# A branch hint that names all five engines, in a kernel of linear attention, routed experts and a gated feed-forward

## The chip, the cores and the metric

The kernel runs on one core of a Trainium2 chip. The metric is the device time of one execution, in microseconds (us). Several runs are made and their median is taken.

## The reference

Three stages follow each other on 1536 tokens (2 sequences of 768) with 384 features:

- attention with a decaying state: for each of 8 heads, `y_t = r_t (state + u k_t v_t)` and then `state = w state + k_t v_t`;
- a mixture of 8 experts, one expert for a token, with a capacity of 384 tokens for an expert: `gate * (relu(x w1) w2)`, inner width 1024;
- a gated feed-forward, `(silu(x w_gate) * (x w_val)) w_out`, inner width 1536.

What the reference computes doesn't limit how many tokens an expert gets, up to its capacity, nor what the decay `w` is. The kernel is written for the usual case of both, and has a second form for the rest.

## The kernel before, in words

The kernel is a straight line of instructions for the usual case: attention in chunks of 128 tokens, experts with at most 224 tokens each (`BLK`), then the gated feed-forward (`gated`, lines 918 to 1004). Behind it, under a condition, stands the general form (`general`, line 1007), which computes everything once more token by token and block by block. The condition is one number, `rare_i`, that VectorE works out in line 829, soon after the routing: it is above 0 when an expert has more than 224 tokens or a decay lies outside 0.6 to 1.6. With the inputs that are timed it is 0, and the general form is jumped over.

The order of each engine's instructions is the order of the source, since the schedule is written by hand (line 78, `manual_schedule`). Where an engine's instruction stands in the source thus decides where it stands in that engine's queue. Each of the five engines has its own stream of instructions, and each of them has to take the same branch for itself: it loads `rare_i` into a register of its own (line 102, TENSOR_LOAD) and compares it (line 107, COMPARE_BRANCH).

The load and the mark for the hint are both in `at_end` (lines 101 to 103). `gated` calls it from line 970, in its last part: the last group of 384 tokens is gated (`inner`), then `outer` takes it in three tiles of 128 tokens. For each tile TensorE makes 36 matmuls into `po` (lines 965 to 967), VectorE adds `po` to `acc` (line 974), and GpSimd scatters the 128 finished rows to `out` (line 976, an indirect DMA through POOL's queue). `at_end` comes between the last tile's matmuls and that tile's addition:

```
967                    nc.tensor.matmul(po, lhsT=al[:, ts_], rhs=wh, start=False, stop=(i == len(parts) - 1))
968                n = g * NTT + tt
969                if n == NT - 1 and last:
970                    at_end()
974                    nc.vector.tensor_add(acc[:, n], acc[:, n], po)
976                    nc.gpsimd.indirect_dma_start(
```

So in TensorE's stream all matmuls stand ahead of the load of the flag, in VectorE's the last addition stands behind it, and in GpSimd's the last scatter does. ScalarE and SyncE (SP, the queue of the plain loads) have no work behind it. At each of these places the compare and branch is the next thing, but for that one addition and that one scatter.

`tc.If` is told to prefer the true branch as the next block (`preferred_fallthrough_block=True`), so the general form stands right behind the straight line in every engine's stream, and the usual case takes the branch over it, to a short block that waits for the last DMAs and to the program's end (line 1143 in the trace).

In the kernel before, line 103 calls `mark_branch_hint_location("rare", hint=0)`. `hint=0` says that the branch labelled `rare` is likely taken. The call names no engine, and the trace has no instruction of line 103 on any of them.

## Time and profile before

| what | value |
|---|---|
| median of 3 runs | 475.48 us (475.33 to 477.2) |
| the profiled execution's own time | 475.25 us |
| its span in the profile | 473.1 us |
| instructions in the span | 8116 |
| mean granted TensorE clock | 0.972 of full speed |
| VectorE, ScalarE, GpSimd busy | 66%, 45%, 38% of the span |

The span goes from the first to the last instruction of the program, and the execution's own time is 2.15 us longer. An engine's name with a "q" behind it (POOLq, PEldq) stands for the engine's sequencer, the part that waits, loads registers, branches and hands instructions on; its time isn't counted as busy. PEld is TensorE's weight load, whose sequencer is TensorE's.

### The profile page before, as it was taken

The page shows a single profiled execution, that of the slowest core. Times are in us where ns is not written, and L with a number is a line of the kernel's source. Part 1 is how long each engine was busy: PE and PEld are TensorE (multiplying, and loading weights), DVE is VectorE, ACT ScalarE, POOL GpSimd, SP SyncE. Part 2 cuts the span into 40 slices and gives each one's busy share as a digit, 9 for nine tenths or more (in the row PEclk, how much of TensorE's full clock was granted, in tenths as well). Part 3 has the DMA queues.
Part 4 walks back from the last instruction along what each step waited for, and adds up shares of the span by engine and source line. Part 5 has one row for each costly group of instructions (what it writes and reads, how often), then busy time and mean ns, then how long its engine had stood idle before and what let it go on. Part 6 is the DMA issues. An engine that isn't in the chain of part 4 may idle for free.

```text
span 473.1 us, 8116 instructions
## 1 busy us (share of the span) xinstructions
PE 448.0 (95%) x3028; PEld 434.8 (92%) x3028; DVE 311.0 (66%) x640; ACT 211.8 (45%) x474; POOL 179.3 (38%) x165
## 2 busy tenths in 40 slices
PE   7898997999999999999999999999999999999991
PEld 6787887889899999999999899999999999999991
DVE  6889899778877878888656787989858111111110
ACT  2556465345666575675554564444343122120310
POOL 6967756121111112010043454755544433233321
PEclk9599799999999999999999999999999999999997
DMA  7785781258989989960201234233310000101001
GB/s 263 245 279 194 247 266 38 74 188 275 346 258 298 234 244 252 303 229 1 68 0 68 78 124 133 73 128 110 100 60 0 34 19 1 51 0 40 11 19 39
DMA packets 24802, 63.78 MB, mean 135 GB/s; under 512 B 4784, under 2 KB 10032, under 8 KB 24752
## 3 DMA queue, kind: packets, MB, share of 16 engines
q1 hardware_dynamic: 22112, 57.43, 38.5%
q0 software_dynamic: 1920, 4.73, 2.8%
q10 hardware_dynamic: 720, 1.00, 0.7%
q8 instruction: 26, 0.43, 0.4%
q14 instruction: 24, 0.20, 0.1%
HBM read 55.67 MB, written 7.48 MB: 133 GB/s over the span
## 4 chain that ended last, share of the span: by engine, by line
PE 79%; DVE 13%; issue 2%; DMA 2%; ACT 1%; POOL 1%; POOLq 0%; DVEq 0%; ACTq 0%
PE A L730 12%; PE py L719 7%; PE g L945 5%; PE g L944 5%; PE g L943 5%; PE A L944 5%; PE A L945 5%; PE A L943 5%; PE po L967 5%; PE po L966 5%; PE po L965 5%; PE py L720 4%; PE A L259 3%; PE A L742 2%; DVE AT L265 2%
## 5 line engine op out<-in xcount | busy, mean ns | idle before, releaser
L952 POOL TENSOR_TENSOR al<-sg,ah 128x384 fp32r<-128x384 f32 x48 | 54.2, 1129 | 122.0 <-ACT ah L951 122.0
L585 DVE TENSOR_TENSOR wlo<-raw,whi 128x768 fp32r<-128x768 f32 x60 | 57.9, 965 | 10.6 <-ACT whi L584 10.0
L719 PE MATMUL py<-hc,whi 128*128 128x448 f32 x192 | 63.1, 370 | 0.0
L951 ACT CAST ah<-sg 128x384 fp32r<-128x384 f32 x48 | 24.7, 514 | 77.8 <-DVE sg L948 77.8
L730 PE MATMUL A<-xc,whi 128*128 128x224 f32 x336 | 57.3, 275 | 0.8 <-DVE xc L601 0.7
L720 PE MATMUL py<-hc,wlo 128*128 128x256 f32 x192 | 53.8, 280 | 0.0
L730 PEld LDWEIGHTS A<-xc,whi 128*128 128x128 f32 x336 | 51.1, 192 | 1.5 <-DVE xc L601 1.1
L584 ACT CAST whi<-raw 128x768 fp32r<-128x768 f32 x60 | 49.9, 838 | 0.7 <-PE py L719 0.7
L966 PE MATMUL po<-w_out_lo,ah 128*128 128x384 f32 x144 | 48.6, 337 | 0.0
L967 PE MATMUL po<-w_out_hi,al 128*128 128x384 f32 x144 | 48.6, 337 | 0.0
L965 PE MATMUL po<-w_out_hi,ah 128*128 128x384 f32 x144 | 48.5, 337 | 0.0
L730 PE MATMUL A<-xc,wlo 128*128 128x224 f32 x168 | 46.2, 275 | 0.0
L974 DVE TENSOR_TENSOR acc<-acc,po 128x384 f32<-128x384 f32 x36 | 19.2, 545 | 30.8 <-PE po L967 30.8
L719 PEld LDWEIGHTS py<-hc,whi 128*128 128x128 f32 x192 | 36.0, 188 | 2.5
L948 DVE TENSOR_TENSOR sg<-A,sg 128x384 f32<-128x384 f32 x24 | 13.3, 555 | 37.9 <-PE A L945 30.2
L720 PEld LDWEIGHTS py<-hc,wlo 128*128 128x128 f32 x192 | 36.5, 190 | 0.0
L795 POOL DMA_INDIRECT ids<-tok,by_expert x12 | 12.1, 1010 | 63.5 <-DMA ids<-tok,by_expert 63.2
L948 DVE TENSOR_TENSOR sg<-g,sg 128x384 f32<-128x384 f32 x24 | 13.3, 555 | 34.5 <-PE g L945 29.7
L253 ACT ACTIVATE AT<-ident,c 128x128 f32<-128x128 f32 x96 | 29.4, 389 | 8.8 <-DVE c L244 8.8
L749 ACT ACTIVATE hc<-A 128x224 fp32r<-128x224 f32 x64 | 23.1, 362 | 21.8 <-PE A L730 18.3
L730 PEld LDWEIGHTS A<-xc,wlo 128*128 128x128 f32 x168 | 32.3, 192 | 0.0
L947 ACT ACTIVATE sg<-A 128x384 f32<-128x384 f32 x24 | 11.7, 487 | 34.6 <-PE A L945 34.6
(166 smaller groups left out, 1185.5 us busy)
## 6 DMA issues: line engine op xcount, KB each, us to landing
raw<-in_w SPq DMA_DIRECT2D x62, 384.0 KB, 6.4
rkT<-in_rkT SPq DMA_DIRECT2D x12, 512.0 KB, 5.0
rk<-in_rk SPq DMA_DIRECT2D x12, 384.0 KB, 4.0
raw<-in_w_gate SPq DMA_DIRECT2D x6, 768.0 KB, 4.2
raw<-in_w_val SPq DMA_DIRECT2D x6, 768.0 KB, 4.3
raw<-in_w_out SPq DMA_DIRECT2D x6, 768.0 KB, 4.3
x_disp<-zero SPq DMA_DIRECT2D x8, 336.0 KB, 6.2
xr<-x_disp SPq DMA_DIRECT2D x8, 336.0 KB, 6.1
```

Source lines behind the costliest of these rows:

```text
L584: nc.scalar.copy(h_, raw)
L585: nc.vector.tensor_sub(l_, raw, h_.bitcast(F32))
L719: nc.tensor.matmul(ps[:, 0:2 * BLK], lhsT=wh, rhs=xc, start=first, stop=False, skip_group_check=True)
L720: nc.tensor.matmul(ps[:, 0:256], lhsT=wl, rhs=xc[:, 0:256], start=False, stop=last, skip_group_check=True)
L730: self.nc.tensor.matmul(ph[:, HI], lhsT=w[:, k, fs], rhs=x[1][:, k, half], start=(k == 0 and i == 0), stop=(k == KD - 1 and i == 2),)
L943: nc.tensor.matmul(pg[m], lhsT=wh[:, k, fs], rhs=xh[:, k], start=(k == 0), stop=False)
L944: nc.tensor.matmul(pg[m], lhsT=wh[:, k, fs], rhs=xl[:, k], start=False, stop=False)
L945: nc.tensor.matmul(pg[m], lhsT=wl[:, k, fs], rhs=xh[:, k], start=False, stop=(k == KD - 1))
L952: nc.gpsimd.tensor_sub(l_, sg, h_.bitcast(F32))
L965: nc.tensor.matmul(po, lhsT=ah[:, ts_], rhs=wh, start=(i == 0), stop=False)
L966: nc.tensor.matmul(po, lhsT=ah[:, ts_], rhs=wl, start=False, stop=False)
L967: nc.tensor.matmul(po, lhsT=al[:, ts_], rhs=wh, start=False, stop=(i == len(parts) - 1))
```

## The change

The hint names all five engines. By the change's own title the finished program then holds it. Nothing else is touched.

```diff
                 def at_end():
                     flag.append(nc.values_load(self.rare_i[0:1, 0:1], min_val=0, max_val=2))
-                    tc.mark_branch_hint_location("rare", hint=0)
+                    tc.mark_branch_hint_location("rare", hint=0, engines=[ET.Pool, ET.PE, ET.DVE, ET.SP, ET.Activation])
```

## Rows read from the trace of the kernel before

**Rows 1.** The page: TensorE's busy time, and the chain that ended last.
```profile
PE 448.0 (95%) x3028; PEld 434.8 (92%) x3028; DVE 311.0 (66%) x640; ACT 211.8 (45%) x474; POOL 179.3 (38%) x165
PE 79%; DVE 13%; issue 2%; DMA 2%; ACT 1%; POOL 1%; POOLq 0%; DVEq 0%; ACTq 0%
```

**Rows 2.** Timeline, last pieces: start us, duration us, engine, line, operation [idle before].
```profile
462.62 0.34 PE L967 MATMUL po<-w_out_hi,al 128*128 128x384 f32 x1
...
462.99 0.55 DVE L974 TENSOR_TENSOR acc<-acc,po 128x384 f32<-128x384 f32 x1 [2.59 <-PE po L967]
```

**Rows 3.** The chain that ended last, from 460 us: start us, duration us, what.
```profile
460.91 3.21 DMA out<-acc,idx
464.12 0.02 issue
464.14 0.02 POOLq L976
464.16 0.51 issue
...
464.89 0.96 POOL out L976
```

**Rows 4.** Line 107, branch and cleanup: ns min/median/max, first and last start us.
```profile
L107 SPq EVENT_SEMAPHORE  x8: 17/17/17, 346.3 to 346.9; - x8
L107 POOLq EVENT_SEMAPHORE  x5: 17/43/2841, 465.1 to 468.3; - x5
L107 DVEq EVENT_SEMAPHORE  x2: 21/21/21, 466.1 to 466.2; - x2
L107 SPq COMPARE_BRANCH  x1: 53/53/53, 342.2 to 342.2; - x1
L107 ACTq COMPARE_BRANCH  x1: 50/50/50, 454.7 to 454.7; - x1
L107 ACTq EVENT_SEMAPHORE  x1: 17/17/17, 457.5 to 457.5; - x1
L107 PEldq COMPARE_BRANCH  x1: 3936/3936/3936, 460.3 to 460.3; - x1
L107 DVEq COMPARE_BRANCH  x1: 72/72/72, 463.0 to 463.0; - x1
L107 PEldq EVENT_SEMAPHORE  x1: 51/51/51, 464.3 to 464.3; - x1
L107 POOLq COMPARE_BRANCH  x1: 45/45/45, 464.7 to 464.7; - x1
L107 POOLq INC_SWDGE_SEM  x1: 904/904/904, 468.4 to 468.4; - x1
```

**Rows 5.** Line 1143, the program's end, same columns.
```profile
L1143 POOLq DRAIN  x3: 40/107/3015, 469.3 to 472.9; - x3
...
L1143 DVEq EVENT_SEMAPHORE  x2: 21/21/21, 472.5 to 473.1; - x2
```

**Rows 6.** Line 102, each engine's load of the flag, same columns.
```profile
L102 SPq TENSOR_LOAD <-rare_i x1: 273/273/273, 341.6 to 341.6; - x1
...
L102 ACTq TENSOR_LOAD <-rare_i x1: 462/462/462, 454.2 to 454.2; - x1
L102 PEldq TENSOR_LOAD <-rare_i x1: 483/483/483, 459.7 to 459.7; - x1
L102 DVEq TENSOR_LOAD <-rare_i x1: 310/310/310, 459.9 to 459.9; - x1
L102 POOLq TENSOR_LOAD <-rare_i x1: 506/506/506, 460.7 to 460.7; - x1
```

**Rows 7.** Line 976, time to landing: all 12 scatters, then the last two alone.
```profile
DMA to landing us min/median/max: 2.6/2.6/3.2
...
DMA to landing us min/median/max: 3.2/3.2/3.2
```

**Rows 8.** Instruction packets while the last two scatters were under way (460.9:464.1, 464.7:468.2).
```profile
q8 instruction: 1, 0.02, 1.9%
...
q8 instruction: 1, 0.02, 2.2%
q14 instruction: 2, 0.02, 1.6%
```

**Rows 9.** The page's DMA queues: packets, MB, share of 16 engines over the span.
```profile
q8 instruction: 26, 0.43, 0.4%
q14 instruction: 24, 0.20, 0.1%
```

## The prediction

> **What bounds the kernel now.** The page comes first: TensorE is busy for 95% of the span, and the chain that ended last runs over it for 79% [rows 1]. Nothing that stands before the hint in any stream is touched, so the question is only what the end of the program waits for. I read that from the last pieces backwards. TensorE's last matmul starts at 462.62, VectorE's last addition runs from 462.99 to 463.54 [rows 2]. Yet the last scatter isn't issued then: GpSimd's sequencer still waits for the landing of the scatter before, at 464.12, and then takes 0.51 us to hand the last one on, which starts at 464.89 [rows 3]. It lands 3.2 us later, about 468.1 [rows 7]. Behind it come GpSimd's cleanup (INC_SWDGE_SEM, 468.4, 0.90 us [rows 4]) and its DRAIN from 469.3 of 3.02 us, to 472.3; only then are the others let go, at 472.5, and the span ends at 473.1 [rows 5]. From 460.9 on the end is a chain of POOL's queue and two scatters; no branch stands on it but GpSimd's own.

> Then the branches. What the hint could save is the time from an engine's branch to its first instruction behind it [rows 4]: SP 342.2 to 346.3, 4.1 us; ScalarE 454.7 to 457.5, 2.8; TensorE 3.94, here inside the branch itself; VectorE 463.0 to 466.1, 3.1; GpSimd 464.7 to 465.1, 0.4. I take the four long ones to be the fetch of the code behind the jump; GpSimd seems to have it at hand.

> **The change, part by part.** It adds one sequencer instruction to each stream, behind the load of the flag, and moves or removes nothing. If the hint starts the fetch at once, an engine gains the time between its hint and its branch:

> - SP, ScalarE and TensorE: the load ends at 341.9, 454.7 and 460.2 [rows 6], and the branch comes at 342.2, 454.7 and 460.3 [rows 4]. The lead is 0.3 us at most, so their waits of 4.1, 2.8 and 3.9 us stay nearly as they are.
> - VectorE: the load ends at 460.2, the branch waits behind the addition until 463.0. The lead of 2.8 us eats nearly the whole 3.1.
> - GpSimd: the load ends at 461.2, the branch comes at 464.7. The lead is 3.5 us, but only 0.4 is there to be saved.

> **What each saving is worth.** All of it ends in a wait. ScalarE, TensorE and VectorE are past the branch at 457.5, 464.3 and 466.1 [rows 4], and their next wait ends at 472.5 [rows 5]; the cover is 6.4 us for the latest of them. SP is past at 346.3 and then waits for the scatters' landings, over 120 us later. GpSimd's first 0.4 us lie inside its wait of 2.84 us for the last landing, which is the long one among the five semaphores [rows 4]. So 0 us for all five, and the cover that would have to go is that of GpSimd, 2.84 us.

> **What the added instructions cost.** The trace has no hint, so I bound it. Its nearest rows are the branches on the same sequencers, 0.045 to 0.072 us where the fetch isn't counted in; the far end is the branch that held its sequencer for 3.94 us [rows 4]. I take 0.05 us, since the hint only hands over the branch's target. At that price it is hidden everywhere. On VectorE it runs in the 2.8 us before the matmuls end, on GpSimd in the 2.9 us from 461.2 to 464.14 in which the sequencer waits for a landing [rows 3]. On TensorE every matmul was handed on before the load, on SP and ScalarE nothing is behind it but the branch. Queued behind the hint and waited for by others are only VectorE's addition (GpSimd waits for it) and GpSimd's scatter (the end does).

> **What the fetches touch.** The last two scatters land after 3.2 us, the median of the twelve is 2.6 [rows 7], and each of the two has a packet of instructions on q8 under way with it, the last one two more on q14 [rows 8]. If these packets are what delays them, moving them matters, and both scatters stand on the chain. The first delay is worth no more than 464.12 - 463.54 = 0.58 us, for then the addition is late next; the second 3.2 - 2.6 = 0.6. The gain is thus between 0 and 1.2 us. I take 0: both windows hold a packet of q8, the queue with the larger packets, and TensorE, the engine with most code, has a lead of only 0.1 us, so that its fetch falls where it fell. An added packet could in turn delay a scatter that isn't delayed now; there is none left among the two, so the bound above is one more delay of the same size, 0.6 us.

> **Sum.** 475.25 us (the profiled execution: 473.1 of span and 2.15 around it) - 0 + 0 = 475.25. The median of the runs is 0.23 above that execution; I give 475.4, between the two, as no change.

> [...] Instruction packets come in two sizes, 0.43 MB / 26 = 16 KB on q8 and 0.20 MB / 24 = 8 KB on q14 [rows 9]; what they displace no row shows. [...]

> **The rivals.**

> - *The change does nothing on the chip*: the instructions stand there, or not, and no fetch starts early. For it: line 103 has no row now. Time 475.4, as forecast. Chance 0.10, told apart only by VectorE's gap.
> - *The moved packets free the scatters*: VectorE's fetches shift by 2.8 us and the last scatter lands in 2.6 us, or both do. 475.25 - 0.6 = 474.65, at most 474.05. For it: 3.2 against 2.6. Against it: q8's packet stays in both windows. Chance 0.18.
> - *The hint holds its sequencer like a fetch*, the lighter one on the slow side. On GpSimd it would run from 461.2 for 3.94 us to 465.15, where the wait ended at 464.14: +1.0 us, 476.3 to 476.5. It decides where the hint takes over 2.9 us. Against it: four of the five branches are recorded at 0.05 to 0.07 us. Chance 0.07.
> - [...] Chance 0.06. [...]
> - *The end waits for code after all*: GpSimd's DRAIN of 3.02 us, or what lies around the span, shrinks as the code comes earlier: over 2.4 us faster, at most 475.25 - 3.0 = 472.2. For it nothing but the size of the DRAIN; it starts right behind a DMA cleanup on the same engine. Chance 0.04.

> **How the numbers follow.** My forecast, nothing moves on the chain, has the remaining 0.55, the rival that does nothing joins it at the same time. 0.5% is 2.4 us, about what a measurement of this kernel can tell from no change. Faster by more needs the last rival and a little of chance: 0.04. Slower by more needs the displaced code, with something for an unforeseen stall at the end: 0.07. The same: 0.89. The range goes from both scatters freed, 474.0, to the held sequencer on top of the median, 475.48 + 1.0, with 0.1 for the added instructions: 476.6. That leaves out the last two cases and little else.

> **What would show it.** Line 103 should have five rows of some 0.05 us: SP near 342, ScalarE near 454.7, TensorE near 460.2, VectorE near 460.2, GpSimd near 461.2. VectorE's first semaphore of line 107 should follow its branch within 0.5 us, not 3.1; TensorE's branch should stay above 3.5 us, SP's and ScalarE's gaps above 2.5. The issue of the last scatter should stay within 0.2 us of where the landing before it puts it, and the DRAIN at 3.0. I am wrong if GpSimd's last scatter starts more than 1 us later against the last matmul, if a hint row is longer than 1 us, or if the stretch from the last landing to the end shrinks.

## The result, and the profile of the changed kernel

The changed kernel is slower: 478.06 us against 475.29 us for the kernel before, medians of 20 runs each, ratio 1.0066 with a 95% interval of 1.0037 to 1.0095. That lies above the range that was given, 474.0 to 476.6 us. Ratios, here and below, leave out the executions over 1.5% above the fastest of their kernel; medians hold all of them. Single executions of either kernel spread widely (471.5 to 480.3 us before, 474.5 to 481.2 after), so that the two profiled ones, with spans of 473.1 and 473.6 us, hardly show the difference; what follows compares stretches inside them, and many runs for the times.

**The hints stand at the wrong end.** The trace has five new instructions. They carry line 1143, not 103, and they run at the very start. Rows of that line in the changed kernel (engine, count: ns min/median/max, first and last start in us):

```profile
L1143 POOLq BRANCH_PREFETCH_HINT  x1: 58/58/58, 0.8 to 0.8; - x1
L1143 ACTq BRANCH_PREFETCH_HINT  x1: 45/45/45, 0.8 to 0.8; - x1
L1143 SPq BRANCH_PREFETCH_HINT  x1: 51/51/51, 0.8 to 0.8; - x1
L1143 DVEq BRANCH_PREFETCH_HINT  x1: 57/57/57, 0.9 to 0.9; - x1
L1143 PEldq BRANCH_PREFETCH_HINT  x1: 50/50/50, 0.9 to 0.9; - x1
```

**What they did to the branches.** Line 107 in the changed kernel answers to [rows 4]:

```profile
L107 SPq EVENT_SEMAPHORE  x8: 17/17/17, 343.7 to 346.7; - x8
L107 POOLq EVENT_SEMAPHORE  x5: 17/43/2312, 466.1 to 468.7; - x5
L107 DVEq EVENT_SEMAPHORE  x2: 21/21/21, 464.7 to 464.8; - x2
L107 SPq COMPARE_BRANCH  x1: 73/73/73, 343.2 to 343.2; - x1
L107 ACTq COMPARE_BRANCH  x1: 68/68/68, 455.8 to 455.8; - x1
L107 ACTq EVENT_SEMAPHORE  x1: 17/17/17, 456.3 to 456.3; - x1
L107 PEldq COMPARE_BRANCH  x1: 482/482/482, 461.3 to 461.3; - x1
L107 PEldq EVENT_SEMAPHORE  x1: 51/51/51, 464.1 to 464.1; - x1
L107 DVEq COMPARE_BRANCH  x1: 84/84/84, 464.1 to 464.1; - x1
```

From the branch to the first instruction behind it: SP 0.5 us instead of 4.1, ScalarE 0.5 instead of 2.8, VectorE 0.6 instead of 3.1. TensorE's branch itself takes 0.48 instead of 3.94, but less was to be gained there: its first instruction behind the branch comes right at the end of the last matmul (464.0) and in the kernel before 1.3 us behind that end (462.96 and 464.3), so that most of the 3.94 us ran beside matmuls. SP's eight semaphores still end 3.5 us behind its branch (343.2 to 346.7; before, 342.2 to 346.9). So a hint given 340 to 460 us ahead does its work: of waits of 2.8 to 4.1 us 0.5 to 0.6 stay. In the profiles below an engine's wait falls like this only where that engine itself has the hint at the start. GpSimd's wait for the last landing is still the long one among its five, 2.31 us. Nothing of the four savings reaches the end, as the prediction had it.

Of the fetches the packets of instructions tell a part. None starts between 0.2 and 20 us in either kernel, so no fetch is seen at the hint (0.8 to 0.9 us). Over the span the changed kernel has fewer than the kernel before [rows 9]:

```profile
q8 instruction: 25, 0.41, 0.4%
q14 instruction: 21, 0.17, 0.1%
```

That is one packet fewer for each of the four engines whose wait is gone, one on q8 and three on q14. In the experiments below SP's hint alone takes one from q14 (23 for 24), and so does ScalarE's; GpSimd's alone takes none; the hints on TensorE, VectorE and ScalarE take one from q8 and two from q14 (25 and 22). So where a hint served, fewer packets came and not more. What it does to the fetches isn't shown: no row says what a packet holds.

**What they did to the start.** The first two loads of SP and ScalarE in the kernel before, and then in the changed one (timeline: start us, duration us, engine, line, operation):

```profile
0.82 0.38 SPq L119 DMA_DIRECT2D w_dm<-in_w_dm  x1
0.83 0.41 ACTq L140 DMA_DIRECT2D u_b<-in_u_row  x1
```

```profile
0.91 0.39 ACTq L140 DMA_DIRECT2D u_b<-in_u_row  x1
0.94 0.38 SPq L119 DMA_DIRECT2D w_dm<-in_w_dm  x1
```

SP was delayed by 0.12 us and ScalarE by 0.08, more than the 0.05 us of the hint's own row, and the order turned round: w_dm (2 KB, the decays) is now issued 30 ns behind u_b (192 KB) instead of 10 ns ahead. The chain of the first 9 us in the changed kernel (start us, duration us, what):

```profile
0.83 0.05 SPq L1143
...
0.94 4.72 DMA w_dm<-in_w_dm
...
5.68 0.17 DVE sq L190
```

and the same stretch of the kernel before:

```profile
0.82 2.53 DMA w_dm<-in_w_dm
...
3.38 0.17 DVE sq L190
```

w_dm takes 4.72 us to land instead of 2.53, and VectorE, which works out the tables of decays from it (line 190 and on), starts 2.3 us later. The hint on SP is itself a link of the chain. In the changed kernel w_dm lands about when u_b does (at 5.66 and 5.5 us). In the kernel before, w_dm's 128 packets of 16 bytes start from 1.81 to 2.12 us, ahead of nearly all of u_b's 128 packets of 1.5 KB (1.93 to 5.24). In the changed kernel they start from 2.18 to 5.18, side by side with u_b's (2.00 to 5.01).

Behind the late tables TensorE's granted clock is lower too. Its matmuls of line 217 are the first to need the tables, behind matmuls that only keep TensorE at work (line 161). Before, and then changed (the bracket is TensorE's idle time ahead of them):

```profile
6.88 0.66 PE L217 MATMUL wps<-ident,W 128*128 128x128 f32 x4 [0.54 <-DVE W L209]
```

```profile
9.98 1.11 PE L217 MATMUL wps<-ident,W 128*128 128x128 f32 x4 [3.41 <-DVE W L209]
```

TensorE idles for 3.41 us instead of 0.54, and from 10 to 15 us the mean granted clock is 0.50 of full speed instead of 0.79. In all six profiles of the document in which line 190 starts at 4.7 us or later, the granted clock falls from full speed to 0.50 of it for the first time between 7.9 and 10.3 us (at 9.6 in the changed kernel); in the other eleven, with line 190 at 3.6 or earlier, between 11.0 and 17.3 (at 12.9 in the kernel before). The executions' mean granted clock follows: 0.967 and 0.968 for the changed kernel in its two sets of runs, 0.967 with SP's hint alone, 0.973 to 0.976 for the kernel before and 0.973 to 0.975 for the four runs below in which the start is repaired. The difference of some 0.0065, over 475 us, is 3.1 us of work at full speed, an estimate from these clocks. That is of the size of the loss, but how much of it lies on the chain no run separates.

**What they did to GpSimd.** A second change is found near 44 us. GpSimd's line 289 (the state's multiplication, 1.0 us) there starts before VectorE's short lines 502 and 512 and not after them. VectorE in the kernel before, and then in the changed one:

```profile
44.15 0.22 DVE L502 SCALAR_TENSOR_TENSOR m<-posall,cap_f,m 128x1 f32<-128x1 f32 x1
44.29 0.15 DVE L512 TENSOR_TENSOR idx<-posall,m 128x1 int32<-128x1 f32 x1
```

```profile
44.40 0.99 POOL L289 TENSOR_TENSOR Z<-zt,Wm 112x384 f32<-112x384 f32 x1 [0.96 <-DVE m L496]
45.36 0.99 POOL L233 TENSOR_TENSOR ruk<-rk 128x384 f32<-128x384 f32 x1
...
44.61 0.83 DVE L502 SCALAR_TENSOR_TENSOR m<-posall,cap_f,m 128x1 f32<-128x1 f32 x1
45.37 1.00 DVE L512 TENSOR_TENSOR idx<-posall,m 128x1 int32<-128x1 f32 x1
```

In the kernel before GpSimd's line 289 starts at 44.31, when line 502 has begun. In the changed one line 502 begins inside line 289 and ends with it (45.44 and 45.39), and line 512 begins and ends with GpSimd's next instruction (46.37 and 46.35). The two lines take 1.83 us together instead of 0.37. No row names what holds VectorE there; what the trace shows is 0.83 us for 0.22 and 1.00 for 0.15, each with its end at the end of GpSimd's instruction. VectorE's line 499, which reads one of its inputs from PSUM, runs beside the same multiplication and takes 0.15 us as before.

### The profile page after: what moved, and what is told of

Read it like the earlier page. It is cut to its first block, busy times and chain, and to the rows that moved or that the text cites. A ratio compares the mean times of both kernels' runs of the same rounds, so it can differ in the third digit from the quotient of the medians.

```text
span 473.6 us, 8121 instructions
## 1 busy us (share of the span) xinstructions
PE 447.7 (95%) x3028; PEld 434.4 (92%) x3028; DVE 316.5 (67%) x640; ACT 211.9 (45%) x474; POOL 182.7 (39%) x165
## 4 chain that ended last, share of the span: by engine, by line
PE 74%; DVE 17%; DMA 3%; issue 2%; ACT 2%; POOL 1%; DVEq 0%; POOLq 0%; SPq 0%; ACTq 0%
PE A L730 11%; PE py L719 7%; PE g L944 5%; PE g L945 5%; PE A L944 5%; PE g L943 5%; PE A L945 5%; PE A L943 5%; PE po L967 5%; PE po L966 5%; PE po L965 4%; PE py L720 4%; DVE RK L228 2%; DVE AT L265 2%; PE A L742 2%
## 5 line engine op out<-in xcount | busy, mean ns | idle before, releaser
L795 POOL DMA_INDIRECT ids<-tok,by_expert x12 | 15.2, 1262 | 61.2 <-DMA ids<-tok,by_expert 60.9
```

## The experiments

Theory A: the order of the loads of w_dm and u_b is the loss. Theory B: what a hint fetches or holds costs in the run. Theory C: each stream is one instruction longer, and its packets of instructions come at other moments. The ratios are against the kernel before on the same chip, with their 95% intervals; every run computes the whole of the reference. Where an edit is to the list of engines, the part of the line that differs from the changed kernel is shown.

**Four hints, none on SP.**

```diff
-engines=[ET.Pool, ET.PE, ET.DVE, ET.SP, ET.Activation]
+engines=[ET.Pool, ET.PE, ET.DVE, ET.Activation]
```

> The hints on four engines, none on SP. In the changed kernel all five hints stand at the start of the streams (0.8 to 0.9 us), and the load of w_dm, which SP issues at 0.94 instead of 0.82, comes behind ScalarE's load of u_b (0.91) and lands after 4.7 us instead of 2.5. Theory A (the order of these two loads is the loss): without SP's hint SP issues at 0.82 again, ahead of ScalarE at 0.91; w_dm lands within 2.7 us, VectorE's first use of it (line 190) stays near 3.4, and the time is that of before, ratio 0.997 to 1.003. Theory B (the code that a hint fetches or holds costs somewhere in the run, on whatever engine): four of five hints remain, ratio 1.004 or more. Theory C (each stream is one instruction longer, and its later blocks of code come at worse moments): as B, 1.004 or more.

Ratio 1.0033 (0.9998 to 1.0068). SP issues w_dm at 0.82, ScalarE u_b at 0.91; w_dm lands after 1.7 us, line 190 starts at 3.2. So the start is repaired, as A has it. The time lies just above A's 0.997 to 1.003 and below B's and C's 1.004, and decides nothing on the rest. By the medians there is no rest: 474.76 us for both.

**The hint on SP alone.**

```diff
-engines=[ET.Pool, ET.PE, ET.DVE, ET.SP, ET.Activation]
+engines=[ET.SP]
```

> The hint on SP alone. Theory A: ScalarE isn't delayed and issues u_b at 0.83, SP issues w_dm at about 0.93, so w_dm is behind by more than in the changed kernel: it lands 4.5 us or more after its issue, VectorE's line 190 starts at 5.5 or later, ratio 1.005 to 1.009. Theories B and C: one hint of five, on the engine with the shortest stream after it, ratio at most 1.002.

Ratio 1.0048 (1.0017 to 1.0079): one hint of five brings most of the loss. The rows are those of A:

```profile
0.83 0.41 ACTq L140 DMA_DIRECT2D u_b<-in_u_row  x1
0.93 0.39 SPq L119 DMA_DIRECT2D w_dm<-in_w_dm  x1
...
L190 DVE TENSOR_SCALAR sq<-w_dm x1: 170/170/170, 5.5 to 5.5; 128x4 f32<-128x4 f32 x1
  DMA w_dm<-in_w_dm: 2.3, 1
```

The last row is VectorE's idle time ahead of line 190, 2.3 us (0.2 in the kernel before).

**Five hints, with u_b as ScalarE's last load.**

```diff
-        nc.scalar.dma_start(out=u_b, in_=a["u_row"].partition_broadcast(P))
 ...
         nc.scalar.dma_start(out=cap_i, in_=a["cap"].bitcast(I32).partition_broadcast(P))
+        nc.scalar.dma_start(out=u_b, in_=a["u_row"].partition_broadcast(P))
```

> All five hints, as in the changed kernel, but ScalarE issues its three loads in the order wg, cap_i, u_b instead of u_b, wg, cap_i, so that u_b's 128 rows of 1.5 KB are issued near 1.8 us, well behind w_dm. Theory A: w_dm lands within 3 us, line 190 starts before 4.0, ratio 0.993 to 1.001, unless u_b itself comes so late that GpSimd's line 234 waits for it. Theories B and C: the hints are as they were, ratio 1.004 or more.

Ratio 1.0030 (0.9999 to 1.0062), w_dm lands after 1.8 us, line 190 at 3.2. As with the four hints: the start is repaired and about 0.3% stays.

**The hint in its place.** With the flag's register as its value the hint must come behind the load of the flag.

```diff
-hint=0, engines=[ET.Pool, ET.PE, ET.DVE, ET.SP, ET.Activation]
+hint=flag[0], engines=[ET.Pool, ET.PE, ET.DVE, ET.SP, ET.Activation]
```

> The hint takes its value from the flag's register instead of the constant 0 (0 is again the likely taken case), so that it can't stand ahead of the load of the flag: on each engine it comes right behind that load, at the place where the prediction took it to be. Theory A and the prediction's sum: the start is as before, line 190 near 3.4, and at the end only waits off the chain get shorter (VectorE's first semaphore of line 107 within 1 us of its branch instead of 3.1); ratio 0.997 to 1.003. Theory B, if the cost of a hint lies in what it fetches and not in where it stands: 1.003 or more. Theory C: streams one instruction longer only at their end, so about 1.000.

Ratio 1.0008 (0.9974 to 1.0042): no difference, as the prediction's sum has it for this place. The rows of VectorE's hint and of two branches, and then the first loads of ScalarE and SP:

```profile
L1143 DVEq BRANCH_PREFETCH_HINT  x1: 61/61/61, 460.3 to 460.3; - x1
...
L107 DVEq EVENT_SEMAPHORE  x2: 21/21/21, 465.9 to 466.0; - x2
L107 DVEq COMPARE_BRANCH  x1: 84/84/84, 463.0 to 463.0; - x1
L107 PEldq COMPARE_BRANCH  x1: 3409/3409/3409, 460.4 to 460.4; - x1
...
0.83 0.41 ACTq L140 DMA_DIRECT2D u_b<-in_u_row  x1
0.83 0.39 SPq L119 DMA_DIRECT2D w_dm<-in_w_dm  x1
```

One part of what was expected failed: VectorE's hint came 2.7 us ahead of its branch, and the first semaphore still followed the branch by 2.9 us, not within 1. In this form the hint saved nothing: VectorE without a hint has 2.9 to 3.2 us there in the other profiles, and the packets of instructions are as many as before, 26 and 24. Whether that is because the hint came late or because its value came from a register, no run separates. In this profile, with no hint at the start, SP issues w_dm 4 ns behind u_b and no longer 10 ns ahead, and w_dm landed after 3.9 us (line 190 at 4.7). In the four profiles in which w_dm is 10 ns ahead it landed after 2.5 to 2.7 us. So even the kernel's own lead of 10 ns isn't sure, and in these profiles the landing follows the order.

**w_dm behind u_b without a hint, and later still.** In the first, w_dm moves to ScalarE's queue behind u_b; in the second it stays on SP, behind the first loads of rkT, rk and v.

```diff
-        nc.sync.dma_start(out=w_dm, in_=a["w_dm"])
 ...
         nc.scalar.dma_start(out=u_b, in_=a["u_row"].partition_broadcast(P))
+        nc.scalar.dma_start(out=w_dm, in_=a["w_dm"])
```

> No hint at all beyond the kernel before; w_dm is issued on ScalarE's queue behind u_b (near 1.27 us) instead of on SP's. Theory A: as in the changed kernel w_dm lands behind u_b's rows, near 5.5 us, line 190 starts at 5.3 to 6, and the time is that of the changed kernel, ratio 1.003 to 1.008, without any hint. Theories B and C: no hint and no longer stream, ratio 0.997 to 1.002 (SP's next loads are even 0.44 us earlier).

```diff
-        nc.sync.dma_start(out=w_dm, in_=a["w_dm"])
 ...
         load_v(0)
+        nc.sync.dma_start(out=w_dm, in_=a["w_dm"])
```

> The dose: no hint, and w_dm issued on SP behind the first loads of rkT, rk and v (near 2.2 us), so that it lands at 8 us or later and line 190 starts some 5 us later than in the kernel before. Theory A: what is lost at line 190 passes through to the end at roughly the share seen for the hint (3 us for 2.3), ratio 1.005 to 1.012, and more than in the run with w_dm behind u_b. The rival (later loads set the pace): the ratio does not grow with the dose, under 1.004.

Ratios 1.0115 (1.0069 to 1.0161) and 1.0190 (1.0137 to 1.0243), both above what was expected. Line 190 starts at 7.8 and 9.4 us, 4.4 and 6.1 later than in the profile of before. The medians rise by 4.5 us (479.53 against 475.07) and 7.6 us (482.67 against 475.07): what is lost at line 190 comes out at the end about whole, and a little over. The mean granted clock falls with it, to 0.969 and 0.959 (0.976 for the kernel before). The rival that later loads set the attention's pace falls.

**u_b last, without a hint; and the hint on ScalarE alone.** The first is the edit of u_b shown above, made in the kernel before. The second:

```diff
-engines=[ET.Pool, ET.PE, ET.DVE, ET.SP, ET.Activation]
+engines=[ET.Activation]
```

> The kernel before, with u_b as ScalarE's last load instead of its first. Theory A: in the kernel before SP's w_dm and ScalarE's u_b are issued 10 ns apart, and w_dm's landing changes from one execution to another (2.5 us in one profile, 3.9 in another with the same start); here it lands within 2 us, line 190 at 3.2, ratio 0.994 to 1.001. The rival, that all small moves at the start come to nothing because later loads set the attention's pace: 0.998 to 1.002 here, and also in the run with w_dm behind.

Ratio 1.0035 (0.9999 to 1.0072). Line 190 at 3.1, and no gain. This is the one result that fits no theory here; its interval holds 1.000, and the later u_b may cost something of its own.

> The hint on ScalarE alone: ScalarE's first load is issued at 0.91, SP's w_dm at 0.82, so w_dm is 90 ns ahead instead of 10. Theory A: w_dm lands within 2 us, line 190 at 3.2, ratio 0.994 to 1.001. Theory B or C: one hint of five, 1.000 to 1.002.

Ratio 1.0017 (0.9981 to 1.0054), w_dm lands after 1.6 us. The ratio is just above A's range and inside B's and C's, and its interval holds them all. With w_dm 80 ns in front nothing is gained over the kernel before, so its 10 ns were mostly enough.

**The changed kernel and the two repaired ones again, side by side.**

> The changed kernel again, beside the next two on one chip, since single executions of any of these kernels spread over some 9 us and 12 runs leave 0.3% of doubt. Theory A: w_dm lands 4.5 us or more after its issue, line 190 near 5.6, ratio 1.004 to 1.009, and its runs average 1.5 to 4 us above those of the two kernels below. Theories B and C: all three are alike within 1 us.

> The four hints without SP's again. Theory A: line 190 at 3.2, ratio 0.997 to 1.003 and 1.5 to 4 us below the changed kernel. Theories B and C: within 1 us of the changed kernel, ratio 1.004 or more.

> All five hints with u_b as ScalarE's last load, again. Theory A: line 190 at 3.2, ratio 0.996 to 1.003, 1.5 to 4 us below the changed kernel. Theories B and C: within 1 us of the changed kernel, ratio 1.004 or more.

Ratios 1.0044 (1.0002 to 1.0086), 1.0026 (0.9992 to 1.0060) and 1.0033 (0.9995 to 1.0070); medians 477.26, 476.01 and 476.63 us. The four hints without SP's are nearer to the kernel before both times: by medians 0.0 and 0.5 us above it, the changed kernel 2.8 and 1.7, though the intervals of the ratios here overlap. Of the 1.5 to 4 us that A expected between the changed kernel and the two repaired ones, the means of all runs show 2.0 and 0.7 (478.06 against 476.05 and 477.32), the second too little. By the ratios a rest of about 0.3% came again with both repairs (by medians 0.5 and 1.1 us), which led to line 289 and to C in a sharper form.

**The hint on GpSimd alone, on neither GpSimd nor SP, and one more GpSimd instruction without a hint.** The edits of the three; the last is made in the kernel before:

```diff
-engines=[ET.Pool, ET.PE, ET.DVE, ET.SP, ET.Activation]
+engines=[ET.Pool]
```

```diff
-engines=[ET.Pool, ET.PE, ET.DVE, ET.SP, ET.Activation]
+engines=[ET.PE, ET.DVE, ET.Activation]
```

```diff
-        for t in kds:
+        for t in kds + kds[2:]:
             nc.gpsimd.memset(t[:, :, D:64], 0.0)
```

> The hint on GpSimd alone. SP and ScalarE issue w_dm and u_b 10 ns apart, as before, so theory A gives the kernel before's time: ratio 0.997 to 1.003. Theory C, sharpened by the traces so far: with one instruction more at the head, GpSimd's stream meets the change to its next block of code (packet on q14 near 41.5 instead of 47.8) while it waits, and not between its wait for zt and the multiplication of line 289; so that multiplication starts 0.12 us after the wait (0.49 in the kernel before), comes ahead of VectorE's lines 502 and 512 and makes these take 0.83 and 1.0 us instead of 0.22 and 0.15. In the six profiles with GpSimd's hint the stretch from the third to the fifth copy of line 320 is 15.9 to 16.5 us, in the seven without 13.0 to 15.0. Expected: 15.9 or more here, the packet near 41.5, ratio 1.001 to 1.004.

> The hints on TensorE, VectorE and ScalarE, on neither SP nor GpSimd: ScalarE's load of u_b 90 ns behind w_dm. Theories A and C (with GpSimd as the only stream where it matters): line 190 at 3.2, GpSimd's packet near 47 to 48 us, the stretch from the third to the fifth copy of line 320 at 13.0 to 15.0, ratio 0.995 to 1.002. Theory B (fetched or held code): three of five hints, 1.002 or more.

> No hint; GpSimd zeroes the third kd buffer twice, so that its stream is one instruction longer from line 170 on, in a stretch where it idles. Theory C: as with GpSimd's hint, packet near 41.5, multiplication of line 289 0.12 us behind its wait, the stretch 15.9 us or more, ratio 1.001 to 1.004. Theory A and B: as the kernel before, stretch 13.0 to 15.0, ratio 0.997 to 1.002.

Ratios 1.0029 (0.9997 to 1.0060), 1.0013 (0.9982 to 1.0043) and 1.0031 (1.0002 to 1.0061); medians 476.87, 475.05 and 476.52 us against 475.45. From the third to the fifth of ScalarE's copies of line 320, one for a chunk of the attention, it takes 16.0, 13.4 and 16.0 us. The same stretch near 44 us with GpSimd's hint alone, without a hint but one instruction more, and with hints on the other three engines:

```profile
44.04 0.99 POOL L289 TENSOR_TENSOR Z<-zt,Wm 112x384 f32<-112x384 f32 x1 [0.96 <-DVE m L496]
...
44.25 0.83 DVE L502 SCALAR_TENSOR_TENSOR m<-posall,cap_f,m 128x1 f32<-128x1 f32 x1
45.01 0.99 DVE L512 TENSOR_TENSOR idx<-posall,m 128x1 int32<-128x1 f32 x1
```

```profile
44.16 0.99 POOL L289 TENSOR_TENSOR Z<-zt,Wm 112x384 f32<-112x384 f32 x1 [0.96 <-DVE m L496]
...
44.37 0.84 DVE L502 SCALAR_TENSOR_TENSOR m<-posall,cap_f,m 128x1 f32<-128x1 f32 x1
45.13 1.00 DVE L512 TENSOR_TENSOR idx<-posall,m 128x1 int32<-128x1 f32 x1
```

```profile
43.59 0.22 DVE L502 SCALAR_TENSOR_TENSOR m<-posall,cap_f,m 128x1 f32<-128x1 f32 x1
43.72 0.15 DVE L512 TENSOR_TENSOR idx<-posall,m 128x1 int32<-128x1 f32 x1
...
43.74 1.00 POOL L289 TENSOR_TENSOR Z<-zt,Wm 112x384 f32<-112x384 f32 x1
```

The collision comes with GpSimd's stream being one instruction longer, be it a hint or a memset, and doesn't come without. All eight profiles with the longer stream have it at this chunk (15.9 to 16.5 us for the stretch), and none of the other nine (13.0 to 15.0). A packet of instructions moves with it: on q14 one packet between 46.5 and 49 us in the kernel before, one between 40 and 43.5 with GpSimd's hint. In the kernel before line 289 starts 0.49 us after its own wait has ended (43.82 and 44.31), with the longer stream 0.12 us (43.92 and 44.04). That the moved packet makes this difference isn't shown: no row names a fetch as what ended the wait.

**A version that keeps the two apart.** In the kernel before, without a hint, the state's update comes behind the routing of the chunk before:

```diff
-            if has_state(it + 1):
-                state_update(it + 1)
             if ok(it - 1):
                 self.route2(it - 1)
+            if has_state(it + 1):
+                state_update(it + 1)
```

> The kernel before with the state's update of a chunk (lines 288 and 289) issued behind the routing of the chunk before it (lines 496 to 516) instead of ahead of it, so that GpSimd's multiplication can't run beside VectorE's lines 502 and 512. If what lengthens these lines is GpSimd's work beside them, they take 0.22 and 0.15 us in most of the 11 chunks, which is worth up to 1.4 us a chunk where they collided: ratio 0.980 to 0.998. If the attention's pace is set elsewhere, 0.998 to 1.003; if the later state holds up the next chunk's outputs, above 1.003.

Ratio 0.9956 (0.9921 to 0.9992), 472.86 against 475.45 us: faster than both kernels. VectorE's lines 502 and 512 over the attention, up to 103 us, in the kernel before, with GpSimd's hint alone, and here (count | busy us, mean ns | idle before):

```profile
L502 DVE SCALAR_TENSOR_TENSOR m<-posall,cap_f,m 128x1 f32<-128x1 f32 x12 | 7.4, 618 | 0.4
L512 DVE TENSOR_TENSOR idx<-posall,m 128x1 int32<-128x1 f32 x12 | 3.5, 292 | 0.0
```

```profile
L502 DVE SCALAR_TENSOR_TENSOR m<-posall,cap_f,m 128x1 f32<-128x1 f32 x12 | 6.8, 566 | 0.4
L512 DVE TENSOR_TENSOR idx<-posall,m 128x1 int32<-128x1 f32 x12 | 6.1, 506 | 0.0
```

```profile
L502 DVE SCALAR_TENSOR_TENSOR m<-posall,cap_f,m 128x1 f32<-128x1 f32 x12 | 3.4, 284 | 0.4
L512 DVE TENSOR_TENSOR idx<-posall,m 128x1 int32<-128x1 f32 x12 | 1.8, 151 | 0.0
```

The two lines together are busy for 10.9, 12.9 and 5.2 us. GpSimd's hint adds 2.0 us there; how much of it is in the time is not shown. The later update takes 5.7 us of busy time away, and the time is 2.6 us shorter. It also moves the state's update itself, so that not all of the 2.6 us need come from the collisions.

## Why the prediction was wrong

**The step that failed is the place.** The prediction says that the change "adds one sequencer instruction to each stream, behind the load of the flag", and that "nothing that stands before the hint in any stream is touched, so the question is only what the end of the program waits for". The hint went near the head of each stream, to 0.8 to 0.9 us, where the prediction had 342 to 461. With that, nearly everything stands behind it, and the whole part on the end answers a question that the change doesn't put. At the price of 0.05 us it calls the hint "hidden everywhere"; ahead of SP's first load it is not, and line 190 starts 2.3 us later. The signs of being wrong that the prediction names look at the end and at the hint's own length, and none of them came true (the last scatter starts 2.1 us behind the start of the last matmul, 2.3 before); only the missing rows of line 103 told.

**What that cost.** Two small shifts at the start, neither among the rivals. SP's hint turns round two loads that are 10 ns apart, and the kernel's first chain waits 2.3 us longer; SP's hint alone is 1.0048, by medians 2.3 us, of the changed kernel's 2.8 and 1.7. GpSimd's hint makes its stream one instruction longer, and a collision with VectorE that the kernel before escapes in some chunks takes place; GpSimd's hint alone is 1.0029, one more instruction without a hint 1.0031. Added, the first two make 1.0077, where the changed kernel measured 1.0066 and 1.0044. The first is shown, by SP's hint alone and, without a hint, by the dose. By which way the lost 2.3 us reach the end, the wait itself or TensorE's lower clock behind it, stays open. Of the second the collision is shown, but not its price: each interval of the 0.3% reaches to about 1.000, the medians give 0.0 to 1.4 us, and the run with u_b last and no hint stands as high (1.0035) without that collision.

**Where the working held.** The length of the hint's row, 0.05 us against 0.044 to 0.061 measured, though SP's first load came 0.12 us later by it; what a hint hands over no row shows. That the four long waits behind the branches are something that a hint can save, though only the packets, one fewer for each, speak for a fetch, and that none of it reaches the end. That a hint behind the flag's load changes nothing in time (1.0008). The forecast that VectorE's wait would go with a lead of 2.8 us was wrong for a late hint (2.9 us stayed): the prediction reckoned with a hint that starts the fetch at once, and in the changed kernel none started at the hint. TensorE's branch, which was to stay above 3.5 us, fell to 0.48, since the lead wasn't 0.1 us but the whole program.

**The rivals.** The hint didn't hold its sequencer: its rows take 0.05 to 0.06 us. A chance of 0.06, and with it the 0.07 for a slower time, went to displaced code, which no run shows: GpSimd's last scatter starts 0.2 us behind its branch in the changed kernel (465.59 and 465.81) as in the one before [rows 3, 4], and the time was lost at the start. The last two scatters landed in 3.0 and 2.7 us instead of 3.2, and from the last matmul to the end it took 9.9 us (463.7 to 473.6) instead of 10.5 [rows 2, 5]; the six other profiles without a hint at the start have 9.7 to 10.0 too, so this is no gain of the hint's. That the change does nothing on the chip is out too: VectorE's gap, which was to tell, fell from 3.1 to 0.6 us, and on SP a hint near the head of the stream took away 3.6 of 4.1 us at a branch 340 us later, and a packet with it.

## What to carry to other kernels

A hint that depends on nothing wasn't placed by where its line stands in the source: look for such an instruction in the stream, above all when the schedule is written by hand, before you ask what hides it. Where two queues issue their first loads within tens of nanoseconds and a small one heads the longest chain, give it a lead by order and not by luck; here that gained nothing, but it keeps the loss away (w_dm landed after 4.7 us at 30 ns behind, after 1.6 to 1.7 at 80 ns ahead). The chain that started late also left TensorE idle early here, 3.41 us instead of 0.54, and the granted clock behind it was 0.50 instead of 0.79, so look at the clock there. And where VectorE's short steps and GpSimd's long ones touched the same moment, a shift of one instruction made the difference between 0.37 and 1.83 us for two of VectorE's lines; the order of the source that keeps them apart was worth 2.6 us here.

## What the runs showed that was not expected

A branch hint given at the start of a 470 us program still served at the branch (0.5 to 0.6 us for 2.8 to 4.1), with no fetch seen at the hint and one packet of instructions fewer for each engine that it served, while one with a register's value, 2.7 us ahead, saved nothing of a 2.9 us wait. A load of 2 KB landed after 4.7 us when it was issued 30 ns behind one of 192 KB on another queue, after 3.9 at 4 ns behind, 2.5 to 2.7 at 10 ns ahead and 1.6 to 1.7 at 80 ns ahead. With it the first fall of TensorE's granted clock moved, from 12.9 to 9.6 us. One more GpSimd instruction at the head of its stream changed two of VectorE's instructions, some 44 us later, from 0.37 to 1.83 us together.
